# The experts' first product by one level of Strassen's algorithm, in two token blocks with the weights loaded for each

## The chip, the cores and the metric

The kernel runs on one core of one Trainium2 chip. The metric is the device time of one execution in microseconds (us), from the first to the last instruction and what lies around them. A program on one core has no other core to wait for. The profile's engines are PE (TensorE, matmul), PEld (its weight loads, which overlap PE), DVE (VectorE), ACT (ScalarE), POOL (GpSimd) and SP (SyncE, which only issues DMAs here).

## What is computed

Three stages in float32. The first is an attention over a small memory, the second a feed-forward layer whose activation is h·cos(h), the third a dense mixture of four experts. Only the third is changed:

```python
def _moe2_ref(x, domain_probs, w1, w2):      # x [2304, 512], w1 [4, 512, 1024], w2 [4, 1024, 512]
    p = domain_probs / (domain_probs.sum(-1, keepdims=True) + 1e-09)
    out = np.zeros((N, D), dtype=np.float32)
    for e in range(E):                        # E = 4
        h = np.maximum(x @ w1[e], 0.0)
        out += p[:, e:e + 1] * (h @ w2[e])
    return out
```

## The kernel before, in words

PE multiplies in float32 by splitting: every operand is held as a high part of reduced precision (`F32R`) and a low part, the rest. `mm3` (L143 to L147) issues three matmuls for one product, high·high, high·low and low·high, so every product below counts three times. The high part is made by an ACT copy, the low part by a subtraction on DVE or POOL (`split`, L101; `split_w`, L105).

**Stage 1** (attention and first feed-forward layer, some 458 us) ends with a loop over slices of the hidden dimension. For each slice and half-sequence `hidden1` (L327) computes `hp` on PE, then the activation goes through ACT, DVE, ACT, DVE and ACT, and at last POOL makes the low part of the tile `gt` (L103). `output1` (L363) multiplies `gt` by `wo`, and DVE adds the product onto `acc` (L380). The output of a unit is issued two units later, which gives the chain time. `acc` holds all 2304 tokens, transposed (d_model on the partitions), in two halves of 1152 tokens.

**Stage 2** (the experts) cuts the hidden dimension of the four experts into 16 slices of 256 and the tokens into 6 blocks of 384. `x1` holds the split of all six blocks, made from `acc` by 24 ACT copies and 24 DVE subtractions (L103, tile `x`) around the end of stage 1. For each slice and block, 96 units in all, `hidden2` (L469) does 2 (halves of the slice) × 4 (quarters of d_model) × 3 matmuls of 384 columns into `hp`, ACT takes the ReLU as the high part (L484), and DVE makes the low part (L485), both for the whole unit of 768 columns. `output2` (L490) then does 3 token tiles × 2 × 3 matmuls of 512 columns into `op`, and DVE scales each by the expert's probability and adds it onto the output (L507), which lies where `acc` lay. The output of a unit is issued behind the hidden product of the next, so PE has other work while ACT and DVE make `ht`. `hp` has two buffers of two PSUM banks, `op` has two tags of two buffers of one bank each.

`load2` (L455) loads a slice's two weight tiles `wa` and `wb` by DMA into `raw` (L116) and splits each: one ACT copy of 1024 columns (L108) and four low parts of 256 columns on POOL (L110). It is called 16 times, each a whole slice ahead. The first two slices are loaded during stage 1: there the DMAs stand in ACT's queue, held back to certain activations (`issue_after`, the list `marks`), and half the low parts are on DVE.

The order of instructions on each engine is set when the program is built, by a list scheduler with a model of its own, from the order of the code, the buffers and `issue_after`. Every engine then takes its own queue strictly in that order.

Of the kernel before, what the change touches and what calls it, by code (L numbers as in the profile page):

```python
# [9 lines left out]
F32 = mybir.dt.float32  # L10
# [14 lines left out]
def tile_kernel(  # L25
# [36 lines left out]
    ps_o = ctx.enter_context(tc.tile_pool(name="ps_o", bufs=2, space=PSUM))  # L62
    ps_a = ctx.enter_context(tc.tile_pool(name="ps_a", bufs=2, space=PSUM))
    c_ctx = ExitStack()
    ps_h = [c_ctx.enter_context(tc.tile_pool(name="ps_h", bufs=2, space=PSUM))]
    ps_c = c_ctx.enter_context(tc.tile_pool(name="ps_c", bufs=2, space=PSUM))
# [74 lines left out]
                op1=ALU.bitwise_or,  # L141
            )

    def mm3(ps, lt, rt, first, last):
        for i, (a, b) in enumerate(((0, 0), (0, 1), (1, 0))):
            nc.tensor.matmul(  # L146
                out=ps, lhsT=lt(a), rhs=rt(b), start=first and i == 0, stop=last and i == 2  # L147
            )

    cs_ctx = ExitStack()  # L150
# [284 lines left out]
            nu += 1  # L435
    wide[0] = True
    c_ctx.close()
    ps_h[0] = ctx.enter_context(tc.tile_pool(name="ps_h2", bufs=2, space=PSUM, reuse_waits="tile"))
# [11 lines left out]
    for p in pend:  # L450
        output1(*p)
    cs_ctx.close()

    x1b = ctx.enter_context(tc.tile_pool(name="x1b", bufs=1, reuse_waits="tile"))
    hg_p = ctx.enter_context(tc.tile_pool(name="hg", bufs=3, reuse_waits="tile"))  # L455
    x1 = [
        (x1b if i else x1a).tile([128, 2, KD, NB], F32R, tag=f"x1_{i}", name="x1") for i in range(NBLK)
    ]

    def load2(s, eng=nc.sync, after=None):  # L460
        e, f0 = s // SPE, (s % SPE) * FS
# [8 lines left out]
        return tiles  # L470

    def hidden2(i, wa):
        hp = ps_h[0].tile([128, NFC, 512], F32, tag="h", name="hp")
        for fc in range(NFC):
            for kk in range(KD):
                mm3(
                    hp[:, fc, :NB],
                    lambda x: wa[:, x, kk, fc * 128:fc * 128 + 128],
                    lambda x: x1[i][:, x, kk, :],
                    kk == 0,  # L480
                    kk == KD - 1,
                )
        ht = hg_p.tile([128, 2, NFC, NB], F32R, tag="hg", name="ht")
        nc.scalar.activation(out=ht[:, 0], in_=hp[:, :, :NB], func=ACTF.Relu)  # L484
        nc.vector.scalar_tensor_tensor(  # L485
            out=ht[:, 1], in0=hp[:, :, :NB], scalar=0.0, in1=f32(ht[:, 0]), op0=ALU.max, op1=ALU.subtract
        )
        return ht

    def output2(s, i, ht, wb):  # L490
        for tt in range(TPB):
            op = (ps_o, ps_a)[tt % 2].tile([128, DM], F32, tag="oa"[tt % 2], name="op")
# [8 lines left out]
            ti = i * TPB + tt  # L501
# [8 lines left out]
            if s == E * SPE - 1:  # L510
                nc.sync.dma_start(out=out[ti * 128:ti * 128 + 128, :], in_=dst)

    for i in range(NBLK):
        u, o = divmod(i * NB, NT // 2)
        with tc.issue_after(marks[(-3, -2, -1, -1, -1, -1)[i]].ins):
            for d in range(KD):
                split(x1[i][:, 0, d], x1[i][:, 1, d], x1v[:, u, d, o:o + NB])

    units = [(s, i) for s in range(E * SPE) for i in range(NBLK)]
# [12 lines left out]


# [28 lines left out]
```

## Time and profile before

| What | Value |
|---|---|
| median of 3 runs (lowest to highest) | 1261.95 us (1261.72 to 1263.91) |
| span of the profiled execution (the page has no other time of it) | 1260.3 us |
| PE, PEld, DVE, ACT, POOL busy, share of the span | 97%, 87%, 54%, 30%, 19% |
| stage 2, from 480 to 1248 us: PE busy | 768.0 of 768.0 us |
| bytes moved by DMA | 55.98 MB, mean 44 GB/s |

Busy is an average over stages. PE's busy time counts matmuls that overlap in its pipeline, so the distance from the start of one group of matmuls to the start of the next is the better measure of what a matmul costs. An order view (below) shows what stands on an engine's queue behind what, and nothing of durations.

### The profile page before, as it was taken

Reading aid. Unit: us, or ns where it says so; the run is one execution under the profiler, and the core shown is the slowest. Engines: PE = TensorE matmul, PEld = TensorE weight load, DVE = VectorE, ACT = ScalarE, POOL = GpSimd, SP = SyncE. Lnnn points to the kernel's source line nnn. Section 1 sums busy time; section 2 is a strip of 40 time slices with the busy share of each in tenths; the row PEclk is TensorE's granted clock in tenths of the full one; section 3 lists DMA queues with packets and bytes.
Section 4 is the critical chain, followed back from the end, with each engine's and each line's share of the span. In section 5 each row is a group of like instructions: output and inputs, shape, how many; then the busy total and the mean of one; then the engine's idle time right before and its main releaser. Section 6 shows DMA issues by size and latency. Waiting matters only on the chain.

```text
span 1260.3 us, 17964 instructions
## 1 busy us (share of the span) xinstructions
PE 1226.7 (97%) x7562; PEld 1096.5 (87%) x7562; DVE 681.8 (54%) x1139; ACT 380.8 (30%) x594; POOL 242.8 (19%) x253
## 2 busy tenths in 40 slices
PE   7788999999999999999999999999999999999998
PEld 5466799999999999889998999889988999899987
DVE  5798989789778873333333333333333333333333
ACT  2466756566556641111111111111111111111010
POOL 1344433333234410010110100101101001001000
PEclk6689999999999999999999999999999999999999
DMA  9953002102212200010100100001001001010012
GB/s 235 237 126 81 19 35 68 37 33 68 68 35 68 68 2 17 17 34 1 34 17 17 34 17 17 34 1 34 17 18 34 17 17 34 1 34 1 1 43 108
DMA packets 35248, 55.98 MB, mean 44 GB/s; under 512 B 2112, under 2 KB 22624, under 8 KB 35168
## 3 DMA queue, kind: packets, MB, share of 16 engines
q1 hardware_dynamic: 28224, 39.07, 11.3%
q10 hardware_dynamic: 6880, 15.73, 4.0%
q8 instruction: 60, 0.98, 0.3%
q14 instruction: 20, 0.16, 0.0%
q0 software_dynamic: 64, 0.04, 0.0%
HBM read 50.11 MB, written 4.72 MB: 44 GB/s over the span
## 4 chain that ended last, share of the span: by engine, by line
PE 90%; DVE 4%; DMA 4%; ACT 1%; issue 0%; SPq 0%; POOL 0%; ACTq 0%; DVEq 0%
PE op L146 47%; PE hp L146 40%; PE vw_ps L314 2%; DMA phi<-in_phi_dram 2%; DMA raw<-in_moe_w_out_dram 1%; DMA q<-in_q_dram 1%; PE kvp L215 1%; PE pq L208 1%; DVE mx L183 1%; DVE gt L103 0%; DVE y L359 0%; DVE kk L354 0%; DVE st L272 0%; DVE wi L135 0%; DVE acc L380 0%
## 5 line engine op out<-in xcount | busy, mean ns | idle before, releaser
L146 PE MATMUL op<-wb,ht 128*128 128x512 f32 x1728 | 418.0, 395 | 1.1 <-ACT ht L484 1.1
L146 PE MATMUL hp<-x,wa 128*128 128x384 f32 x2304 | 416.2, 336 | 0.0
L146 PEld LDWEIGHTS hp<-x,wa 128*128 128x128 f32 x2304 | 402.7, 188 | 8.6
L146 PEld LDWEIGHTS op<-wb,ht 128*128 128x128 f32 x1728 | 323.5, 188 | 70.3 <-ACT ht L484 1.3
L485 DVE SCALAR_TENSOR_TENSOR ht<-hp,ht 128x768 fp32r<-128x768 f32 x96 | 91.9, 958 | 400.0 <-ACT ht L484 400.0
L484 ACT ACTIVATE ht<-hp 128x768 fp32r<-128x768 f32 x96 | 77.8, 812 | 632.3 <-PE hp L146 632.3
L507 DVE SCALAR_TENSOR_TENSOR acc<-op,p_all,acc 128x512 f32<-128x512 f32 x270 | 201.9, 748 | 89.3 <-PE op L146 89.3
L146 PE MATMUL op<-gt,wo 128*128 128x288 f32 x1536 | 227.6, 298 | 3.2 <-DVE vw L103 2.0
L146 PEld LDWEIGHTS op<-gt,wo 128*128 128x128 f32 x1536 | 211.0, 189 | 8.8 <-DVE gt L103 1.9
L110 POOL TENSOR_TENSOR wa<-raw,wa 128x256 fp32r<-128x256 f32 x60 | 43.4, 754 | 507.4 <-ACT wa L108 507.4
L146 PE MATMUL hp<-attnT,vw 128*128 128x288 f32 x768 | 130.4, 305 | 5.2 <-DVE y L359 2.8
L146 PEld LDWEIGHTS hp<-attnT,vw 128*128 128x128 f32 x768 | 110.5, 192 | 18.8 <-issue 12.8
L103 POOL TENSOR_TENSOR gt<-y,gt 128x576 fp32r<-128x576 f32 x52 | 80.5, 1547 | 174.2 <-ACT gt L102 143.2
L380 DVE TENSOR_TENSOR acc<-op,acc 128x288 f32<-128x288 f32 x224 | 96.3, 449 | 19.6 <-PE op L146 19.2
L110 POOL TENSOR_TENSOR wb<-raw,wb 128x256 fp32r<-128x256 f32 x60 | 43.2, 751 | 132.7 <-ACT wb L108 132.7
L358 ACT ACTIVATE y<-y 128x576 f32<-128x576 f32 (+1 forms) x76 | 46.2, 609 | 64.4 <-DVE y L350 51.3
L102 ACT ACTIVATE gt<-y 128x576 fp32r<-128x576 f32 (+1 forms) x76 | 46.0, 606 | 38.2 <-DVE y L359 38.0
L359 DVE TENSOR_TENSOR y<-hp,y 128x576 f32<-128x576 f32 (+1 forms) x76 | 49.6, 653 | 5.9 <-ACT y L358 5.8
L347 ACT ACTIVATE y<-hp 128x576 f32<-128x576 f32 (+1 forms) x76 | 42.9, 568 | 14.4 <-PE hp L146 14.1
L350 DVE SCALAR_TENSOR_TENSOR y<-kk,y 128x576 f32<-128x576 f32 x52 | 42.4, 815 | 4.8 <-ACT kk L349 4.2
L314 PE MATMUL vw_ps<-wi,vz 128*32 128x256 f32 x512 | 37.2, 401 | 2.1 <-DVE wi L135 2.1
L349 ACT ACTIVATE kk<-y 128x576 f32<-128x576 f32 x52 | 35.6, 685 | 1.4
(82 smaller groups left out, 617.0 us busy)
## 6 DMA issues: line engine op xcount, KB each, us to landing
raw<-in_moe_w_dram SPq DMA_DIRECT2D x28, 512.0 KB, 3.5
raw<-in_moe_w_out_dram ACTq DMA_DIRECT2D x14, 512.0 KB, 3.5
raw<-in_moe_w_in_dram ACTq DMA_DIRECT2D x12, 512.0 KB, 3.7
kv<-in_k_dram SPq DMA_DIRECT2D x16, 288.0 KB, 5.6
kv<-in_v_dram SPq DMA_DIRECT2D x16, 288.0 KB, 6.8
q<-in_q_dram SPq DMA_DIRECT2D x8, 576.0 KB, 7.6
out_dram<-acc SPq DMA_DIRECT2D x18, 256.0 KB, 2.0
phi<-in_phi_dram SPq DMA_DIRECT2D x8, 288.0 KB, 7.8
```

What stands on the lines that cost most here:

```text
L102: nc.scalar.activation(out=hi, in_=src, func=ACTF.Copy)
L103: (eng or nc.vector).tensor_tensor(out=lo, in0=src, in1=f32(hi), op=ALU.subtract)
L110: (nc.vector if early and c % 512 else nc.gpsimd).tensor_tensor(out=t[:, 1, c:c + 256], in0=src[:, c:c + 256], in1=f32(t[:, 0, c:c + 256]) ...
L146: nc.tensor.matmul(out=ps, lhsT=lt(a), rhs=rt(b), start=first and i == 0, stop=last and i == 2)
L314: nc.tensor.matmul(out=vw_ps[32 * i:32 * i + 32, g, :], lhsT=vz[b][:, g, i, :], rhs=wi[:, 2 * g + i // 2, :], start=True, stop=True,)
L347: marks.append(nc.scalar.activation(out=y, in_=hv, func=ACTF.Copy, scale=INV_2PI, bias=0.25))
L358: nc.scalar.activation(out=y, in_=y, func=ACTF.Sin, scale=-TWO_PI if wide[0] else TWO_PI)
L359: nc.vector.tensor_tensor(out=y, in0=hv, in1=y, op=ALU.mult)
L380: nc.vector.tensor_tensor(out=dst, in0=op[:, :TH], in1=dst, op=ALU.add)
L484: nc.scalar.activation(out=ht[:, 0], in_=hp[:, :, :NB], func=ACTF.Relu)
L485: nc.vector.scalar_tensor_tensor(out=ht[:, 1], in0=hp[:, :, :NB], scalar=0.0, in1=f32(ht[:, 0]), op0=ALU.max, op1=ALU.subtract)
L507: nc.vector.scalar_tensor_tensor(out=dst, in0=op, scalar=pe, in1=dst, op0=ALU.mult, op1=ALU.add)
```

## The change

Tokens: instead of six blocks of 384, the tokens are taken as two blocks (u) of 1152, and all 16 slices are run for the first block before the second begins. So the weights are loaded and split 32 times instead of 16. Each block has two groups (j) of 512 and 640 tokens; a unit is one slice and one group, 64 units in all.

Products: for a unit the group's tokens are halved (n = 256 or 320), d_model is halved, and the slice is halved. The 2×2×2 half-size products, 8 by the direct way, are made from 7 by Strassen's algorithm in Winograd's form. The seven left operands of a slice (three quarters of the weights and four combinations) are made in `load2`: four POOL subtractions and seven low parts, all of 256 columns on POOL, three ACT copies. The seven right operands of a group (three quarters of x and four combinations) are made by `build_x`: four DVE combinations, seven ACT copies, seven DVE low parts, each of 2n columns. The sums are taken on the way out: ACT copies the first product out of PSUM, DVE does five additions, and two products are accumulated in PSUM onto banks (`ba`, `b5`) that were already read once. The ReLU and the low parts are taken in three pieces.

PSUM: `hp` and `op` get pools of their own, 5 banks for products and 3 for outputs, in place of the four kinds above.

The diff, cut to its core:

```diff
-    def mm3(ps, lt, rt, first, last):
+    def mm3(ps, lt, rt, first, last, more=False):
...
-    x1a = ctx.enter_context(tc.tile_pool(name="x1a", bufs=1, side="right", reuse_waits="tile"))
...
+    SUBS = ((0, 256), (512, 320))
+    xp = ctx.enter_context(tc.tile_pool(name="xp", bufs=1, reuse_waits="tile"))
+    tp = ctx.enter_context(tc.tile_pool(name="tp", bufs=2, reuse_waits="tile"))
+    hg_p = ctx.enter_context(tc.tile_pool(name="hg", bufs=2, reuse_waits="tile"))
+
+    def build_x(u, j, after=None):
+        t0, n = SUBS[j]
+        xv = x1v[:, u]
+        a11, a12 = xv[:, 0:2, t0:t0 + n], xv[:, 2:4, t0:t0 + n]
+        a21, a22 = xv[:, 0:2, t0 + n:t0 + 2 * n], xv[:, 2:4, t0 + n:t0 + 2 * n]
...
+        def put(o, src):
+            x = xp.tile([128, 2, 2, n], F32R, tag=f"x{j}_{o}", name=f"x{j}_{o}")
+            nc.scalar.activation(out=x[:, 0], in_=src, func=ACTF.Copy)
+            nc.vector.tensor_tensor(out=x[:, 1], in0=src, in1=f32(x[:, 0]), op=ALU.subtract)
+            ops[o] = x
+
+        with tc.issue_after(after.ins) if after else nullcontext():
+            put(0, a11)
+            s1 = comb("sA", a21, a22, ALU.add, nc.vector)
+            s2 = comb("sB", s1, a11, ALU.subtract, nc.vector)
+            put(5, s2)
+            s3 = comb("sC", a11, a21, ALU.subtract, nc.vector)
+            put(6, s3)
+            put(4, s1)
+            put(3, a22)
+            put(1, a12)
+            s4 = comb("sA", a12, s2, ALU.subtract, nc.vector)
+            put(2, s4)
...
     def load2(s, eng=nc.sync, after=None):
...
+            pool.tensor_tensor(out=tt[:, 0], in0=b12, in1=b11, op=ALU.subtract)
+            pool.tensor_tensor(out=tt[:, 1], in0=b22, in1=tt[:, 0], op=ALU.subtract)
+            pool.tensor_tensor(out=tt[:, 2], in0=b22, in1=b12, op=ALU.subtract)
+            pool.tensor_tensor(out=tt[:, 3], in0=b21, in1=tt[:, 1], op=ALU.subtract)
...
+            for o, src in enumerate((b11, b21, b22, tt[:, 0], tt[:, 1], tt[:, 2], tt[:, 3])):
+                pool.tensor_tensor(out=wa[:, 1, o], in0=src, in1=f32(wa[:, 0, o]), op=ALU.subtract)
...
+    PROD = {1: (0, 0), 2: (1, 1), 3: (2, 2), 4: (6, 3), 5: (3, 4), 6: (4, 5), 7: (5, 6)}
...
+        ba = bank()
+        prod(ba, 1)
+        p1 = tmp("p1")
+        nc.scalar.copy(out=p1, in_=ba[:, :n])
+        b6 = bank()
+        prod(b6, 6)
+        u2 = tmp("u2")
+        add(u2, b6, p1)
+        b7 = bank()
+        prod(b7, 7)
+        u3 = tmp("u3")
+        add(u3, b7, u2)
+        b5 = bank()
+        prod(b5, 5)
+        add(c[:, 1, n:], b5, u3)
+        b4 = bank()
+        prod(b4, 4)
+        add(c[:, 0, n:], b4, u3)
+        prod(ba, 2, True)
+        nc.scalar.activation(out=ht[:, 0, 0, :n], in_=ba[:, :n], func=ACTF.Relu)
...
+        prod(b5, 3, True)
+        add(c[:, 1, :n], b5, u2)
...
+    units = [(u, s, j) for u in range(NU) for s in range(NS2) for j in range(2)]
...
+    ps_p = ctx.enter_context(tc.tile_pool(name="ps_p", bufs=5, space=PSUM, reuse_waits="tile"))
+    ps_q = ctx.enter_context(tc.tile_pool(name="ps_q", bufs=3, space=PSUM, reuse_waits="tile"))
+    for u, s, j in units:
+        q_ = u * NS2 + s
+        if j == 1 and 0 < q_ < NU * NS2 - 1:
+            w[q_ + 1] = load2((q_ + 1) % NS2)
+        ht = hidden2(j, xo[u, j], w[q_][0])
+        if u + 1 < NU and s == NS2 - 1:
+            xo[u + 1, j] = build_x(u + 1, j)
```

Three places of the order follow. Numbers behind a name tell buffers apart; line numbers of the change are its own.

**PE in the middle of stage 2.** Before, a unit is one run of 24 matmuls for `hp` and three output tiles of the unit ahead:

```order
L146 MATMUL hp_5823<-x1_5331,wa_5401 128x384 x24
L146 MATMUL op_5851<-wb_5409,ht_5796 128x512 x6
L146 MATMUL op_5859<-wb_5409,ht_5796 128x512 x6
L146 MATMUL op_5867<-wb_5409,ht_5796 128x512 x6
L146 MATMUL hp_5875<-x1_5332,wa_5401 128x384 x24
```

Now a unit of the larger group (`x1_0` to `x1_6` are its seven right operands):

```order
L147 MATMUL hp_6192<-x1_0_5358,wa_5941 128x320
L147 MATMUL hp_6201<-x1_5_5365,wa_5941 128x320 x2
L147 MATMUL op_6156<-wb_5732,ht_5965 128x512 x6
L147 MATMUL hp_6201<-x1_5_5365,wa_5941 128x320 x4
L147 MATMUL hp_6210<-x1_6_5370,wa_5941 128x320 x6
L147 MATMUL hp_6219<-x1_4_5373,wa_5941 128x320 x6
L147 MATMUL hp_6227<-x1_3_5376,wa_5941 128x320 x6
L147 MATMUL hp_6192<-x1_1_5379,wa_5941 128x320 x6
L147 MATMUL op_6254<-wb_5958,ht_6061 128x512 x6
L147 MATMUL op_6262<-wb_5958,ht_6061 128x512 x6
L147 MATMUL hp_6219<-x1_2_5384,wa_5941 128x320 x6
L147 MATMUL op_6270<-wb_5958,ht_6061 128x512 x6
```

Between the fifth product (into `hp_6219`, the bank `b5`) and the last, which accumulates onto that bank, stand two products and two output tiles.

**DVE at the handover from stage 1 to stage 2.** Before, the low parts of the first blocks stand among the last additions onto `acc`; these are the rows around the last four of them:

```order
L380 TENSOR_TENSOR acc_73<-op_5288,acc_73 128x288
L380 TENSOR_TENSOR acc_73<-op_5296,acc_73 128x288
L103 TENSOR_TENSOR x1_5333<-acc_73,x1_5333 128x384
L380 TENSOR_TENSOR acc_73<-op_5304,acc_73 128x288
L103 TENSOR_TENSOR x1_5334<-acc_73,x1_5334 128x384
L380 TENSOR_TENSOR acc_73<-op_5312,acc_73 128x288
```

Now all of `build_x` stands behind the last addition:

```order
L386 TENSOR_TENSOR acc_73<-op_5309,acc_73 128x288
L476 TENSOR_TENSOR sA_5332<-acc_73 128x512
L476 TENSOR_TENSOR sC_5339<-acc_73 128x512
L484 TENSOR_TENSOR x0_0_5329<-acc_73,x0_0_5329 128x512
L476 TENSOR_TENSOR sB_5334<-sA_5332,acc_73 128x512
L484 TENSOR_TENSOR x0_3_5347<-acc_73,x0_3_5347 128x512
L484 TENSOR_TENSOR x0_1_5350<-acc_73,x0_1_5350 128x512
L484 TENSOR_TENSOR x1_0_5358<-acc_73,x1_0_5358 128x640
L484 TENSOR_TENSOR x1_3_5376<-acc_73,x1_3_5376 128x640
L484 TENSOR_TENSOR x1_1_5379<-acc_73,x1_1_5379 128x640
L484 TENSOR_TENSOR x0_4_5344<-sA_5332,x0_4_5344 128x512
L484 TENSOR_TENSOR x0_6_5341<-sC_5339,x0_6_5341 128x512
```

The first product waits for `x0_0`, which has moved behind two combinations; before, its operands were ready long ahead of the last addition.

**POOL near the end of stage 1**, where it also makes the low part of every `gt`. Before:

```order
L110 TENSOR_TENSOR wa_5401<-raw_5399,wa_5401 128x256 x2
L103 TENSOR_TENSOR gt_4904<-y_4902,gt_4904 128x576
L103 TENSOR_TENSOR gt_4971<-y_4969,gt_4971 128x576
L110 TENSOR_TENSOR wb_5409<-raw_5407,wb_5409 128x256 x2
L103 TENSOR_TENSOR gt_5026<-y_5024,gt_5026 128x576
```

Now (`gt_4901`, `gt_4968` and `gt_5023` are the same three tiles; three combinations of `tt_5415` stand ahead of the first row):

```order
L527 TENSOR_TENSOR wa_5416<-raw_5413,wa_5416 128x256 x3
L516 TENSOR_TENSOR tt_5415<-raw_5413,tt_5415 128x256
L104 TENSOR_TENSOR gt_4901<-y_4899,gt_4901 128x576
L527 TENSOR_TENSOR wa_5416<-tt_5415,wa_5416 128x256 x4
L104 TENSOR_TENSOR gt_4968<-y_4966,gt_4968 128x576
L513 TENSOR_TENSOR tt_5714<-raw_5712 128x256
L515 TENSOR_TENSOR tt_5714<-raw_5712 128x256
L514 TENSOR_TENSOR tt_5714<-raw_5712,tt_5714 128x256
L111 TENSOR_TENSOR wb_5433<-raw_5431,wb_5433 128x256 x2
L516 TENSOR_TENSOR tt_5714<-raw_5712,tt_5714 128x256
L104 TENSOR_TENSOR gt_5023<-y_5021,gt_5023 128x576
```

The combinations of the third slice (`tt_5714`) have moved in front of `gt_5023`, and their `raw_5712` shares its buffer with `raw_5413`.

## Rows read from the trace of the kernel before

**Rows 1.** Windows by stage: busy us, instructions, clock (PEclk), DMA share, GB/s.
```profile
30.00:60.00 30.00, 22.75 (x187) 14.94 (x179) 23.84 (x53) 14.27 (x30) 12.05 (x15) 0.57 0.95 231
...
458.00:480.00 22.00, 20.93 (x111) 18.88 (x110) 12.32 (x22) 6.43 (x12) 0.00 (x0) 1.00 0.00 1
480.00:1248.00 768.00, 768.00 (x3861) 693.75 (x3860) 286.72 (x368) 102.07 (x119) 79.23 (x112) 1.00 0.07 23
```

**Rows 2.** Chain that ended last, first and last units: start us, us, what.
```profile
483.14 4.24 PE hp L146 x24
487.38 4.19 PE op L146 x18
...
1243.86 4.16 PE hp L146 x24
1248.02 8.41 PE op L146 x36
```

**Rows 3.** Timeline of PE, 222 to 227 us: start us, us, engine line op.
```profile
222.62 3.35 PE L146 MATMUL op<-gt,wo 128*128 128x288 f32 x24
225.81 0.96 PE L146 MATMUL hp<-attnT,vw 128*128 128x288 f32 x6
```

**Rows 4.** Timeline of PEld and PE, 104 to 128 us: six transposes.
```profile
122.39 0.60 PEld L208 LDWEIGHTS pq<-ident,q 96*128 96x128 f32 x6
122.52 0.66 PE L208 MATMUL pq<-ident,q 96*128 96x96 f32 x6
```

**Rows 5.** Page, part 5: weight loads of the experts' first product.
```profile
L146 PEld LDWEIGHTS hp<-x,wa 128*128 128x128 f32 x2304 | 402.7, 188 | 8.6
```

**Rows 6.** Groups on DVE by line, 100 to 460 us.
```profile
L380 DVE TENSOR_TENSOR acc<-op,acc 128x288 f32<-128x288 f32 x222 | 95.4, 449 | 19.6 <-PE op L146 19.2
L135 DVE SCALAR_TENSOR_TENSOR wi<-raw 128x512 uint32<-128x512 uint32 x12 | 14.5, 1217 | 0.3
L135 DVE SCALAR_TENSOR_TENSOR wf<-raw 128x512 uint32<-128x512 uint32 x12 | 8.2, 687 | 0.2
```

**Rows 7.** Page, part 5: DVE's largest groups in stage 2.
```profile
L485 DVE SCALAR_TENSOR_TENSOR ht<-hp,ht 128x768 fp32r<-128x768 f32 x96 | 91.9, 958 | 400.0 <-ACT ht L484 400.0
...
L507 DVE SCALAR_TENSOR_TENSOR acc<-op,p_all,acc 128x512 f32<-128x512 f32 x270 | 201.9, 748 | 89.3 <-PE op L146 89.3
```

**Rows 8.** Groups on POOL by line: 395 to 435 us, then 480 to 1248 us.
```profile
L103 POOL TENSOR_TENSOR gt<-y,gt 128x576 fp32r<-128x576 f32 x8 | 11.6, 1444 | 12.2 <-issue 12.2
L110 POOL TENSOR_TENSOR wb<-raw,wb 128x256 fp32r<-128x256 f32 x4 | 3.7, 950 | 5.6 <-ACT wb L108 5.6
...
L110 POOL TENSOR_TENSOR wa<-raw,wa 128x256 fp32r<-128x256 f32 x56 | 39.7, 741 | 502.8 <-ACT wa L108 502.8
```

**Rows 9.** Timeline of PE at the handover.
```profile
445.89 4.33 PE L146 MATMUL hp<-x,wa 128*128 128x384 f32 x24
...
453.26 3.46 PE L146 MATMUL hp<-x,wa 128*128 128x384 f32 x19
...
457.95 2.80 PE L146 MATMUL op<-gt,wo 128*128 128x288 f32 x20
461.82 0.50 PE L146 MATMUL op<-wb,ht 128*128 128x512 f32 x1 [1.07 <-ACT ht L484]
```

**Rows 10.** Timeline of DVE, 457 to 466 us: low parts of `x`.
```profile
464.21 1.95 DVE L103 TENSOR_TENSOR x<-acc,x 128x384 fp32r<-128x384 f32 x4
```

**Rows 11.** Timelines, 415 to 462 us: ACT, POOL, then PE.
```profile
420.94 1.06 ACT L108 ACTIVATE wa<-raw 128x1024 fp32r<-128x1024 f32 x1 [1.40 <-DMA raw<-in_moe_w_dram]
...
423.89 1.43 POOL L103 TENSOR_TENSOR gt<-y,gt 128x576 fp32r<-128x576 f32 x1
...
427.08 3.35 PE L146 MATMUL op<-gt,wo 128*128 128x288 f32 x24
...
437.83 3.36 PE L146 MATMUL op<-gt,wo 128*128 128x288 f32 x24
```

**Rows 12.** Page, part 6: loads of the experts' weights in stage 2.
```profile
raw<-in_moe_w_dram SPq DMA_DIRECT2D x28, 512.0 KB, 3.5
```

More of the change, by code (lines that the diff above doesn't have):

```diff
@@ L142, in narrow @@
             )
-    def mm3(ps, lt, rt, first, last):
+    def mm3(ps, lt, rt, first, last, more=False):
         for i, (a, b) in enumerate(((0, 0), (0, 1), (1, 0))):
             nc.tensor.matmul(
-                out=ps, lhsT=lt(a), rhs=rt(b), start=first and i == 0, stop=last and i == 2
+                out=ps,
+                lhsT=lt(a),
+                rhs=rt(b),
+                start=first and i == 0,
+                stop=last and i == 2,
+                skip_group_check=more,
             )
@@ L437, in tile_kernel @@
     c_ctx.close()
-    ps_h[0] = ctx.enter_context(tc.tile_pool(name="ps_h2", bufs=2, space=PSUM, reuse_waits="tile"))
+    ps_h[0] = p_ctx.enter_context(tc.tile_pool(name="ps_h2", bufs=2, space=PSUM, reuse_waits="tile"))
     load_probs()
@@ L470, in load2 @@
[L470 to L487, printed above, removed]
-        return ht
@@ L490, in output2 @@
-    def output2(s, i, ht, wb):
-        for tt in range(TPB):
-            op = (ps_o, ps_a)[tt % 2].tile([128, DM], F32, tag="oa"[tt % 2], name="op")
+        early = after is not None
+        raw = wc.tile([128, KD, FS], F32, tag="raw", name="raw")
+        with tc.issue_after(after[0].ins) if early else nullcontext():
+            eng.dma_start(out=raw, in_=w1[e, :, f0:f0 + FS].rearrange("(k p) f -> p k f", p=128))
+        b11, b12 = raw[:, 0:2, 0:128], raw[:, 0:2, 128:256]
+        b21, b22 = raw[:, 2:4, 0:128], raw[:, 2:4, 128:256]
@@ new lines, in load2, with hidden2, prod, bank @@
+        with tc.issue_after(after[1].ins) if early else nullcontext():
+            wb = load_split("wb", w2[e, f0:f0 + FS, :].rearrange("(k p) d -> p k d", p=128), [NFC, DM], eng, early)
+        return wa, wb
+    PROD = {1: (0, 0), 2: (1, 1), 3: (2, 2), 4: (6, 3), 5: (3, 4), 6: (4, 5), 7: (5, 6)}
+    def hidden2(j, xo, wa):
+        n = SUBS[j][1]
+        def prod(bank, i, more=False):
+            wo_, xo_ = PROD[i]
+            for kk in range(2):
+                mm3(
+                    bank[:, :n],
+                    lambda x: wa[:, x, wo_, kk, :],
+                    lambda x: xo[xo_][:, x, kk, :],
+                    not more and kk == 0,
+                    kk == 1,
+                    more,
+                )
+        def bank():
+            return ps_p.tile([128, 512], F32, tag="p", name="hp")
+        def tmp(tag):
+            return tp.tile([128, n], F32, tag=tag, name=tag)
+        def add(out, ps, sb):
+            nc.vector.tensor_tensor(out=out, in0=ps[:, :n], in1=sb, op=ALU.add)
+        c = tp.tile([128, NFC, 2 * n], F32, tag="c", name="c")
+        ht = hg_p.tile([128, 2, NFC, 2 * n], F32R, tag="hg", name="ht")
+        ba = bank()
[18 more added lines that the diff above has]
+        nc.scalar.activation(out=ht[:, 0, 0, :n], in_=ba[:, :n], func=ACTF.Relu)
+        nc.vector.scalar_tensor_tensor(
+            out=ht[:, 1, 0, :n], in0=ba[:, :n], scalar=0.0, in1=f32(ht[:, 0, 0, :n]), op0=ALU.max, op1=ALU.subtract
+        )
+        prod(b5, 3, True)
+        add(c[:, 1, :n], b5, u2)
+        for fc, lo in ((0, n), (1, 0)):
+            nc.scalar.activation(out=ht[:, 0, fc, lo:], in_=c[:, fc, lo:], func=ACTF.Relu)
+            nc.vector.scalar_tensor_tensor(
+                out=ht[:, 1, fc, lo:],
+                in0=c[:, fc, lo:],
+                scalar=0.0,
+                in1=f32(ht[:, 0, fc, lo:]),
+                op0=ALU.max,
+                op1=ALU.subtract,
+            )
+        return ht
@@ L493, in output2 @@
+    def output2(u, s, j, ht, wb):
+        t0, n = SUBS[j]
+        for tt in range(2 * n // 128):
+            op = ps_q.tile([128, DM], F32, tag="q", name="op")
             for fc in range(NFC):
@@ L509, in output2 @@
                 )
-            if s == E * SPE - 1:
+            if s == NS2 - 1:
                 nc.sync.dma_start(out=out[ti * 128:ti * 128 + 128, :], in_=dst)
[L513 to L519, printed above, removed]
+    xo = {(0, j): build_x(0, j, marks[(-3, -1)[j]]) for j in range(2)}
+    units = [(u, s, j) for u in range(NU) for s in range(NS2) for j in range(2)]
     w = {}
```

49 lines of the change are left out of this document (29 added, 20 removed).

## The prediction

> **What bounds the kernel now.** The windows by stage come first [rows 1]. From 480 to 1248 us PE is busy for all of 768.00 us at a granted clock of 1.00, which is its 2.4 GHz level, while DVE works 286.72, ACT 102.07 and POOL 79.23 us and the DMA engines 7%. The reader is to see there that no other engine is near PE, and that the only loss nearby is 1.07 us between 458 and 480. The chain of work that ended last [rows 2] says the same in order of time: `hp`, `op`, `hp`, `op`, each released by the one before. From the `hp` at 483.14 to that at 1243.86 are 91 units of 8.36 us; `op` takes 4.19 of them, so `hp` 4.17. So stage 2 is a sum of matmul distances. Fewer columns shorten it one for one, every new wait of PE lengthens it one for one, and the 480 to 690 us that DVE, ACT and POOL are idle there are what the change can spend.
>
> **The products.** A matmul of 384 columns costs 4.17/24 = 173.8 ns, one of 512 columns 4.19/18 = 232.8 ns. Stage 1 has a third width [rows 3]: 24 matmuls of 288 columns in 225.81 − 222.62 = 3.19 us, 132.9 ns each. At 2.4 GHz 384 and 288 columns alone would take 160 and 120 ns, so about 13 ns stay on each matmul whatever its width. The line through these two has 0.426 ns a column; it gives 146.5 ns for 320 columns (between two rows) and 119.3 ns for 256, which no row shows. For 256 the bounds are 106.7 ns (the columns alone) and 132.9 ns (no shorter than 288). I take 119.3, because the 13 ns are the same at both narrow widths. Weight loads are no floor above that: six transposes with loads of 128 columns finish in 0.66 us, at most 110 ns each [rows 4].
>
> Removed: 96 × 4.17 = 400.3 us. Added: 32 slices × 7 products × 6 matmuls × (119.3 + 146.5 ns) = 1344 × 265.8 = 357.2 us. That is **−43.1 us** (bounds −60 and −25). The output keeps its 1728 matmuls of 512 columns: 0.
>
> Weight loads are busy for 693.75 of the 768 us [rows 1], and those of this product for 402.7 us in 2304 loads, 174.8 ns each [rows 5]. The Trainium skill (Perfetto Trace Analysis, Identifying the Most-Contended Engine) says to judge how near TensorE is to its limit by just this share and not by the matmuls' busy time. If these loads were the limit, 2688 of them would take 469.8 us, and the term would be +69.5 instead of −43.1. Against it stand the 24 loads of rows 3, one every 132.9 ns, so I keep −43.1.
>
> **In the middle of stage 2** PE gets new partners. A slice now lasts 11.2 us (products) plus 54 × 232.8 ns = 12.6 us (outputs), 23.7 us. DVE's work in it: five additions per unit at 449 ns for 288 columns [rows 6], scaled by columns 5 × (0.40 + 0.50) = 4.5 us; low parts of 4 × 576 columns at 958/768 = 1.25 ns a column, 2.9 us; nine output additions of 748 ns, 6.7 us [rows 7]. Together 14.1 of 23.7 us. POOL's 15 operations of 741 ns [rows 8] are 11.1 us, and their result is wanted a slice later. The one close wait is the bank `b5`: its second product may start only when DVE has read the first. Between them stand two products and two output tiles, 2 × 0.72 + 2 × 1.40 = 4.2 us for the smaller group, against one addition of 0.4 us. So I cost it at 0; the cover is those 4.2 us, and each us beyond it would cost 64 us. An output tile takes 1.40 us, its evacuation 0.75, so three banks are enough.
>
> **The handover.** Before, two whole `hp` units stood among the last outputs of stage 1 [rows 9] and hid the end of its activation chain, all but the 1.07 us. Now no product can start before DVE has finished the last addition onto `acc` and then two combinations and the low part of `x0_0`, and DVE's queue for the first slice holds 22 operations of 512 or 640 columns. Four of 384 columns took 1.95 us [rows 10], 1.27 ns a column: 0.65 and 0.81 us, 16 us in all. Going through the two queues from the end of the last addition (t = 0, PE idle since −0.65): `x0_0` is ready at 1.95, PE waited 2.6. Product 6 wants the high part of `x0_5`, behind `sB` and an ACT copy, 3.15: 0.5. PE then has three single matmuls, products 4 and 2, until 4.95; the low part of `x0_4` stands behind three operations of 640 columns and is ready at 6.95: 2.0. With products 5, 7, 6 and the first products of the second group PE reaches 12.0; the high part of `x1_5` is ready at 14.95: 2.9. Its low part, 17.1, costs another 1.1. After that DVE stays ahead. Sum 9.1 us, against 1.07 before: **+8.0 us**. Bounds: +1.5 (only the first wait is real) and +15 (nothing of the 16 us is hidden). The idle could also bring the clock down: between 30 and 60 us, with PE busy for 22.75 of 30, the granted clock was 0.57 [rows 1]; that is inside the upper bound.
>
> **The end of stage 1.** POOL made 4 low parts per slice of weights there, now 13 operations; beside a busy DVE one takes 950 ns [rows 8]. Before, the weights of the second slice were there at 420.94, the low part of `gt` for the output at 427.08 was made from 423.89 to 425.3, 1.8 us early [rows 11]. Now seven operations, 6.7 us, stand ahead of it: from 421.3 to 428.0, and with its own 1.44 us 429.4, 2.1 us late. Four more end at 433.1. Only then is `raw` free for the third slice, whose load takes 3.5 us [rows 12], and POOL's queue waits for it with six operations ahead of `gt_5023`: 436.7 + 5.7 + 1.4 = 443.8. The output that wants it starts at 437.83 [rows 11], now 2.1 later, and can do two or three matmuls on the high part: 440.2. So 3.6 more, **+5.7 us** (bounds 0 and 12).
>
> DVE's operation on `wi`, always beside POOL, takes 1217 ns, the same on `wf` 687 [rows 6], and POOL's own 950 against 741 [rows 8]. The Trainium skill (SBUF — State Buffer, SBUF: two separate sides) says that a VectorE operation with two SBUF inputs and a GpSimd operation lock each other out of a shared port for a whole instruction. By that, some of the longer POOL queue would also delay DVE's part of the activation chain, about 3 us in all, and the term would be 8.7; in the middle of stage 2, at most four such operations a slice would leave DVE at 17 of 23.7 us. I keep 5.7.
>
> **The second block.** Its `build_x` (16 us of DVE) falls into some 31 us of PE work that bring DVE some 18 us of their own, but three of the combinations are made ahead. I take **+1 us** (0 to 5). The end is unchanged: 1260.3 less the last matmul's 1256.43 [rows 2].
>
> **Sum.** −43.1 + 8.0 + 5.7 + 1 = −28.4. From the span of 1260.3 that is 1231.9; the median of the runs lies 1.65 above that span, so **1233.5 us**. From no change a measurement here tells about 0.2%, 2.5 us.
>
> **Rivals.**
> - *The distance does not fall below that of 288 columns.* 256 columns at 132.9 ns: the products cost 375.5, the sum is −10.1, 1252 us. For it: no row is narrower at full clock with this operand. Against: the equal 13 ns and rows 4.
> - *The edges are nearly free*, since list order lets POOL and DVE catch up: handover +1.5, the others 0. The sum is −41.6, 1220 us. Against: the queues are strict, and their lengths are counted.
> - *Slower: PE waits on `b5` in each unit.* If DVE's queue comes so late that the addition ends more than 4.2 us after product 5, every unit waits. It decides from 28.4/64 = 0.45 us per unit; at 1 us the time is 1233.5 + 64 = 1297. For it: DVE's queue interleaves output additions with the chain, and POOL can hold it up. Against: 14.1 of 23.7 us, and 10 times the time needed.
> - *Slower by the loads.* At 174.8 ns a load the sum is +84, 1344 us. Rows 3 speak against.
>
> **Chances.** The forecast, with its edges anywhere from half to one and a half of what I took (1226 to 1241) and the distance within some 5 ns, 70%. Narrow floor 10%. Free edges 10%. Waits on `b5` 7%, loads 2%, others 1%. The range 1217 to 1254 takes in the first three. Faster by over 0.2%: 88%. Within it: 3%, the narrow floor with dear edges. Slower: 9%.
>
> **What would show it.** Right: 32 × 42 matmuls of 256 and 320 columns at 119 and 146 ns start to start, PE busy without a gap from some 490 us to the end but for a us near the middle, idle PE of 9 us behind the last stage-1 output with DVE's `x` tiles named, and idle PE before outputs near 427 and 440 us with POOL's `gt` named. Wrong: one distance for both widths; a gap in every unit with a releaser on DVE; or no gap at the edges.

## The result, and the profile after

The changed kernel takes 1223.49 us (median of 4 runs, 1220.88 to 1227.39), the kernel before 1261.84 us in the same comparison. The ratio is 0.9703, with a 95% interval of 0.9678 to 0.9728: 38.4 us less, where 28.4 were forecast. The profiled execution has a span of 1222.8 us, against 1260.3 before.

The first 300 us differ by some us from profile to profile. So the parts are compared from a fixed point, the start of the 24th activation from the end of stage 1 (ACT, L347 before and L353 now, at 319.61 and 319.13 us; between 317.0 and 325.9 us in the thirteen profiles of this case). From there the span lasts 940.7 us before and 903.7 us now, 37.0 less. A second profile of the changed kernel gives 902.8, so this measure is good to about 1 us. Where a stretch is measured to or from an addition, its start is meant.

**Steady state.** The page's lines of the changed kernel on PE's busy time and on the loads of the first product. PE is busy for 97% as before; the product has 2688 loads and as many matmuls, before 2304 [rows 5]:

```profile
PE 1189.1 (97%) x7946; PEld 1055.3 (86%) x7946; DVE 868.3 (71%) x1571; ACT 486.4 (40%) x854; POOL 525.3 (43%) x609
...
L147 PEld LDWEIGHTS hp<-x,wa 128*128 128x128 f32 x2688 | 381.2, 189 | 25.8 <-DVE x L484 3.0
```

The chain of work that ended last, of the changed kernel, one slice (start us, us, what):

```profile
589.81 2.80 PE op L147 x12
592.61 0.88 PE hp L147 x6
...
603.29 0.70 PE hp L147 x6
...
613.47 2.80 PE op L147 x12
```

It is PE all the way, as in [rows 2]. A slice lasts 613.47 − 589.81 = 23.66 us. Six matmuls of 320 columns take 0.88 us, 147 ns each, six of 256 take 0.70, 117 ns each.

**The handover.** The same chain where stage 1 ends:

```profile
449.36 3.05 PE op L147 x21
452.41 0.02 issue
452.43 0.46 DVE acc L386
452.89 0.60 DVE sA L476
453.49 0.60 DVE sC L476
454.09 0.60 DVE x L484
...
465.19 0.74 DVE sB L476
465.93 0.02 issue
465.95 0.75 ACT x L483
466.70 0.04 issue
466.74 6.18 PE hp L147 x30
```

Here the chain leaves PE: from 452.43 to 465.93 us it goes through DVE's queue. Between the fixed point and PE's last matmul it does so only once more, for one addition of 0.47 us at 448.84. PE's timeline in that stretch names what it waited for (idle us and releaser in brackets; five waits, 4.40 us in all, of which two rows). The third row is ACT's, ahead of the copy `p` that the second wait names: ACT, too, was waiting for DVE.

```profile
454.74 0.85 PE L147 MATMUL hp<-x,wa 128*128 128x256 f32 x5 [2.01 <-DVE x L484]
...
465.39 1.16 PE L147 MATMUL hp<-x,wa 128*128 128x320 f32 x6 [1.32 <-ACT p L564]
...
464.29 0.74 ACT L483 ACTIVATE x<-sA 128x640 fp32r<-128x640 f32 x1 [1.66 <-DVE sA L476]
```

In windows (columns as in [rows 1]), and behind them one slice:

```profile
455.00:460.00 5.00, 4.12 (x23) 3.63 (x23) 5.00 (x9) 1.28 (x3) 0.00 (x0) 0.69 0.00 0
460.00:465.00 5.00, 4.07 (x26) 3.44 (x25) 5.00 (x9) 2.09 (x4) 0.00 (x0) 0.97 0.00 0
465.00:470.00 5.00, 4.41 (x18) 4.04 (x19) 5.00 (x10) 2.56 (x6) 0.00 (x0) 0.71 0.00 0
470.00:475.00 5.00, 5.00 (x36) 4.87 (x35) 4.50 (x10) 1.17 (x3) 0.00 (x0) 0.95 0.01 3
613.47:637.13 23.66, 23.66 (x139) 21.21 (x139) 14.72 (x25) 6.50 (x13) 11.41 (x15) 1.00 0.15 45
```

DVE is busy throughout, and the granted clock, 1.00 until 455 us, fell behind the waits to 0.69 and 0.71, that is to 1.2 GHz for a part of these windows. That is 5 × (0.31 + 0.03 + 0.29 + 0.05) = 3.4 us of PE's full speed. In the second profile of the change the waits are 4.34 us and the clock takes only 5 × (0.07 + 0.27) = 1.7 us, from 450 to 460 us.

**The end of stage 1.** POOL's timeline, then SP's (the issue of the third slice's load), then PE's (two outputs):

```profile
419.48 0.74 POOL L513 TENSOR_TENSOR tt<-raw 128x256 f32<-128x256 f32 x1 [0.61 <-DMA raw<-in_moe_w_dram]
...
424.89 1.44 POOL L104 TENSOR_TENSOR gt<-y,gt 128x576 fp32r<-128x576 f32 x1
...
431.00 0.73 POOL L513 TENSOR_TENSOR tt<-raw 128x256 f32<-128x256 f32 x1
...
436.17 1.44 POOL L104 TENSOR_TENSOR gt<-y,gt 128x576 fp32r<-128x576 f32 x1
...
424.96 0.38 SPq L506 DMA_DIRECT2D raw<-in_moe_w_dram  x1
...
426.47 3.34 PE L147 MATMUL op<-gt,wo 128*128 128x288 f32 x24
...
437.20 3.63 PE L147 MATMUL op<-gt,wo 128*128 128x288 f32 x24
```

The low parts are ready at 426.33 and 437.61. The first is in time by 0.14 us. The second is late by 0.41, but the output can begin on the high part, and its 24 matmuls take only 0.27 us longer than before [rows 11].

**The sum**, from the fixed point: products −45.5 (32 × 23.66 = 757.1 for 96 × 8.36 = 802.6), end of stage 1 +0.1 (133.3 us to the last addition; before 141.6, with 8.4 of stage 2's products among it), handover +7.8 (766.5 us from the last addition to PE's end less 757.1 and less the middle, 8.9, against 1.07 before), middle +0.5. Together −37.1. Of the 8.9 us of the handover the waits and the clock make 7.8.

### The profile page after: what moved, and what is told of

Read it like the earlier page. It is cut to its first block, busy times and chain, and to the rows that moved or that the text cites. A ratio compares the mean times of both kernels' runs of the same rounds, so it can differ in the third digit from the quotient of the medians.

```text
span 1222.8 us, 20022 instructions
## 1 busy us (share of the span) xinstructions
PE 1189.1 (97%) x7946; PEld 1055.3 (86%) x7946; DVE 868.3 (71%) x1571; ACT 486.4 (40%) x854; POOL 525.3 (43%) x609
## 4 chain that ended last, share of the span: by engine, by line
PE 89%; DVE 6%; DMA 3%; ACT 1%; issue 0%; POOL 0%; SPq 0%; DVEq 0%
PE op L147 48%; PE hp L147 37%; PE vw_ps L320 2%; DMA phi<-in_phi_dram 2%; DMA q<-in_q_dram 1%; PE kvp L221 1%; DMA raw<-in_moe_w_out_dram 1%; DVE x L484 1%; PE pq L214 1%; DVE mx L189 1%; DVE gt L104 0%; DVE y L365 0%; DVE st L278 0%; DVE acc L386 0%; DVE kk L360 0%
## 5 line engine op out<-in xcount | busy, mean ns | idle before, releaser
L147 PE MATMUL op<-wb,ht 128*128 128x512 f32 x1728 | 439.3, 396 | 0.0
L147 PEld LDWEIGHTS hp<-x,wa 128*128 128x128 f32 x2688 | 381.2, 189 | 25.8 <-DVE x L484 3.0
L147 PE MATMUL hp<-x,wa 128*128 128x320 f32 (+1 forms) x2688 | 394.2, 296 | 4.4 <-DVE x L484 2.5
L111 POOL TENSOR_TENSOR wb<-raw,wb 128x256 fp32r<-128x256 f32 x124 | 90.1, 758 | 225.5 <-ACT wb L109 225.4
L587 ACT ACTIVATE ht<-c 128x256 fp32r<-128x256 f32 (+3 forms) x128 | 72.0, 562 | 285.7 <-DVE c L557 285.7
L588 DVE SCALAR_TENSOR_TENSOR ht<-c,ht 128x256 fp32r<-128x256 f32 (+3 forms) x128 | 95.2, 743 | 63.5 <-ACT ht L587 63.5
L527 POOL TENSOR_TENSOR wa<-raw,wa 128x256 fp32r<-128x256 f32 x96 | 71.6, 773 | 150.1 <-ACT wa L517 150.1
L557 DVE TENSOR_TENSOR c<-hp,u 128x256 f32<-128x256 f32 (+1 forms) x192 | 87.4, 457 | 42.3 <-PE hp L147 37.9
L527 POOL TENSOR_TENSOR wa<-tt,wa 128x256 fp32r<-128x256 f32 x128 | 108.1, 875 | 0.0
L564 ACT COPY p<-hp 128x256 f32<-128x256 f32 x64 | 25.6, 400 | 109.5 <-PE hp L147 109.4
```

Of the source, the lines that this page charges most:

```text
L111: (nc.vector if early and c % 512 else nc.gpsimd).tensor_tensor(out=t[:, 1, c:c + 256], in0=src[:, c:c + 256], in1=f32(t[:, 0, c:c + 256]) ...
L147: nc.tensor.matmul(out=ps, lhsT=lt(a), rhs=rt(b), start=first and i == 0, stop=last and i == 2, skip_group_check=more,)
L527: pool.tensor_tensor(out=wa[:, 1, o], in0=src, in1=f32(wa[:, 0, o]), op=ALU.subtract)
L557: nc.vector.tensor_tensor(out=out, in0=ps[:, :n], in1=sb, op=ALU.add)
L587: nc.scalar.activation(out=ht[:, 0, fc, lo:], in_=c[:, fc, lo:], func=ACTF.Relu)
L588: nc.vector.scalar_tensor_tensor(out=ht[:, 1, fc, lo:], in0=c[:, fc, lo:], scalar=0.0, in1=f32(ht[:, 0, fc, lo:]), op0=ALU.max, op1=ALU.su ...
```

## The experiments

All are edits of the changed kernel; from the combinations on POOL on, a run keeps edits of earlier runs, as its expectation says, and its cut shows the new ones alone. "Handover" is the time from the last addition of stage 1 to the first ReLU of slice 3, the slices counted from 0 (the expectations call it the third slice); 77.3 and 76.3 us in the two profiles of the change.

### Eight products in place of seven

```diff
-        prod(ba, 1)
-        p1 = tmp("p1")
...
+        for fc in range(NFC):
+            for h in range(2):
+                hp = bank()
+                for kk in range(KD):
+                    mm3(
+                        hp[:, :n],
+                        lambda x: wa[:, x, kk, fc * 128:fc * 128 + 128],
+                        lambda x: xo[2 * h + kk // 2][:, x, kk % 2, :],
+                        kk == 0,
+                        kk == KD - 1,
+                    )
```

> All 8 half-size products in place of 7, with the same two token blocks, widths, banks and twice loaded weights, and no combinations. If the gain of the change is the products that it saves (A), a slice has 96 product matmuls for 84: at the 117 and 147 ns measured in the change, 32 x 12 x 132 ns = +50.7 us in stage 2, and some 4 us less at the handover, since only 8 low parts are made there: about 1269 us, 0.5% above the kernel before. If the gain came from the new order of blocks, banks or tiles and not from the saved products (B), the time stays near the change's 1223 us. The idle PE at the handover should fall below 3 us with this shorter DVE queue.

Measured: 1274.33 us (1.0107 of before, 1.0081 to 1.0133). Its chain, the first row of one slice and the same row of the next, and the one wait of its PE at the handover:

```profile
610.63 4.20 PE op L147 x18
...
635.88 4.20 PE op L147 x18
```

```profile
454.90 1.33 PE L147 MATMUL op<-gt,wo 128*128 128x288 f32 x4 [6.57 <-ACT gt L103]
```

A slice lasts 25.25 us, 1.59 more than with seven products, 50.9 us in 32 slices. So theory A holds: the gain is the saved products. The new blocks and widths alone cost 32 × 25.25 − 802.6 = +5.4 us; leaving out the eighth product gives 50.9 back. The expectation missed at the handover: ACT's queue had the eight copies of `x`, and DVE's the eight low parts, ahead of the last unit's activation chain, and PE waited 6.6 us for that.

### Narrower and wider products

```diff
-    SUBS = ((0, 256), (512, 320))
+    SUBS = ((0, 192), (384, 384))
```

To make room, the tile `c` loses its unused quarter, and two small constants of stage 1 move to a pool that is released.

> The change, with groups of 384 and 768 tokens in place of 512 and 640, so the half-size products have 192 and 384 columns. If a matmul costs a fixed share per column (A: 117 ns for 256, 147 for 320, 173.8 for 384 are all 0.45 to 0.46 ns a column), 192 columns take 88 ns and the time stays within 2 us of the change's. If some 13 ns stay on each matmul whatever its width (B, the prediction's reading), 192 columns take 93 ns and 384 some 173: the same sum, told apart by the distance alone. If the loads of 128 columns set a floor near the 110 ns that the transposes bound (C), 1344 matmuls take 110 for 88 ns: +30 us, 1252.

Measured: 1254.83 us (0.9962, 0.9944 to 0.998). Its chain:

```profile
600.34 3.33 PE hp L137 x30
...
604.39 0.65 PE hp L137 x6
...
622.27 1.04 PE hp L137 x6
...
624.94 3.33 PE hp L137 x30
```

Six matmuls of 192 columns take 0.65 us, 108 ns each, and 30 take 3.33, 111 ns each; 384 columns take 1.04/6 = 173 ns. A slice lasts 24.60 us, 0.94 more: 30 us in all, the size that C gave. From 256 columns on the price is proportional: 0.456 ns a column at 256, 0.458 at 320, 0.451 at 384. At 192 the distance is 108 to 111 ns in place of the 88 that this would give, so the products of the change, at 117 ns, stand just above it.

That the load of the weights sets this distance is argued, not shown: no run changed the load alone. The Trainium skill (TensorE: Matmul & The Clock Gate, LDWEIGHTS (loading the stationary operand)) gives a load of P columns as P/1.2 ns whatever the rows, an estimate of 107 for 128: the products of this run come close to it. But the six transposes of [rows 4], each with a load of 128 columns in 96 rows, do not agree: one matmul of theirs lasts 0.25 us, so six in 0.66 us start (0.66 − 0.25)/5 = 0.082 us apart. A load of 128 columns does not hold every matmul to 107 ns.

The weight loads' busy share, which the Trainium skill (Perfetto Trace Analysis, Identifying the Most-Contended Engine) takes as a measure, does not tell the two apart: 21.21 of 23.66 us (90%) in the change, 22.23 of 24.60 (90%) here, where half of the products stand some 20 ns farther apart than their columns would give.

### More work on POOL at the end of stage 1

```diff
+            for _ in range(2 if early else 0):
+                pool.tensor_tensor(out=tt[:, 2], in0=b22, in1=b12, op=ALU.subtract)
+                pool.tensor_tensor(out=tt[:, 3], in0=b21, in1=tt[:, 1], op=ALU.subtract)
```

> Four more POOL subtractions (some 0.71 us each, the same values written again) in the two loads of weights during stage 1, ahead of the low parts of the output's tile gt. If POOL's queue is as close to what PE waits for there as the change's trace looks (low part ready at 426.33 for an output at 426.47, and at 437.61 for one at 437.20) (A), 2.8 us more cost 2 to 3 us at each of two or three outputs, +5 to +9 us in all. If the queue has slack that the walk missed (B), the time stays within 1 us.

Measured: 1227.06 us (0.9729, 0.9703 to 0.9756); from the fixed point to the last addition 137.9 us in place of 133.3, +4.6. PE's timeline shows idle time where there was none:

```profile
415.75 0.37 PE L147 MATMUL op<-gt,wo 128*128 128x288 f32 x1 [1.91 <-DVE acc L386]
...
439.73 0.37 PE L147 MATMUL op<-gt,wo 128*128 128x288 f32 x1 [0.72 <-DVE acc L386]
```

The size fits A, a little under its 5 to 9; from the fixed point to the end it is 3.6 us, since the handover is 76.3. The chain that ended last ran on PE there in the change, but for the one addition; here POOL's low parts and combinations are its largest part from 424 to 451 us. But PE did not wait for `gt`, as A had it. The releaser is DVE's addition, which frees the output's bank, and ahead of it stands an operation of the activation that took 1.96 us, with POOL busy beside it; the shortest of its kind in the change took 0.74:

```profile
413.27 1.96 DVE L356 SCALAR_TENSOR_TENSOR y<-kk,y 128x576 f32<-128x576 f32 x1
```

PE's two waits are 2.63 us. Behind the first the granted clock was 0.67 from 415.8 to 421 us, some 1.7 us of full speed, so both make 4.3 of the 4.6 us. The program's order around these outputs changed with the edit, so the single waits are not laid at one tile's door.

### The bank b5, freed later

```diff
-        add(c[:, 1, n:], b5, u3)
+        for _ in range(5):
+            add(c[:, 1, n:], b5, u3)
```

> The addition that frees bank b5 for its second product is made five times in place of once, 64 times over. DVE gets 4 x (0.37 + 0.44) = 3.2 us more in a slice, 18 of 23.7 us, and the bank is free 1.5 to 1.8 us later. If the cover of 4.2 us between the two products on that bank holds (A), the time stays within 2.5 us of the change's 1223. If the bank or DVE's queue is close to what PE waits for (B), each unit is longer by up to 1.6 us, +100 us; 0.2 us a unit would already be +13.

Measured: 1226.29 us (0.9721, 0.9695 to 0.9748). In the window from 520 to 800 us:

```profile
520.00:800.00 280.00, 280.00 (x1636) 250.99 (x1635) 206.55 (x389) 77.51 (x141) 134.75 (x176) 1.00 0.15 46
```

DVE does 206.55 us of work where the change has 174.56, and PE is still busy for all of 280.00; a slice lasts 23.64 us. A holds: in the steady state the cover is there. From the fixed point it is 2.4 us more, of which 1.1 lie at the second block, where DVE also builds the new `x`.

### Work for PE in the first wait

```diff
+    end1 = mm[0]
...
+    idle = ps_q.tile([128, DM], F32, tag="q", name="idle")
+    with tc.issue_after(end1.ins):
+        for _ in range(9):
+            nc.tensor.matmul(out=idle[:, :128], lhsT=ones, rhs=ones, start=True, stop=True)
```

> The change, with nine matmuls of 128 columns on constants put into PE's queue behind the last matmul of stage 1, that is into the 2.0 us in which PE waits for the first low part of x. Their result is not used. If the 3.4 us that the lower clock costs behind the handover (granted 0.69 to 0.97 from 455 to 475 us) are a cost of their own, brought by the idle PE (A), the clock stays up and the time falls by some 3 us. If DVE's queue sets the end of the handover (B), PE gets faster only to wait longer for the next low parts: more idle time, a higher clock, the same end within 1 us.

Measured: 1221.88 us (0.9692, 0.9662 to 0.9721). Windows, then PE's timeline:

```profile
455.00:460.00 5.00, 3.49 (x24) 3.15 (x25) 5.00 (x9) 0.79 (x3) 0.00 (x0) 1.00 0.00 0
...
465.00:470.00 5.00, 4.34 (x29) 4.26 (x30) 4.87 (x10) 2.29 (x4) 0.00 (x0) 1.00 0.02 3
```

```profile
458.55 0.86 PE L149 MATMUL hp<-x,wa 128*128 128x256 f32 x5 [1.31 <-DVE x L487]
...
465.66 3.76 PE L149 MATMUL hp<-x,wa 128*128 128x320 f32 x25 [1.61 <-ACT x L486]
```

The clock stays at 1.00, so it was the idle PE that brought it down. Of the 3.4 us, 1.9 come back (handover 75.3 for 77.3), or 1.0 of 1.7 against the second profile; the rest turns into longer waits for `x` (the two rows, 1.31 for 0.46 and 1.61 for 0.20). Both theories are half right: DVE's queue sets most of the end, the clock a part. In the time of the whole run the intervals overlap with the change's, so no gain is shown there.

### The first operands built earlier

```diff
+    bx0 = build_x(0, 0)
+    next(bx0)
+    for p in pend:
+        output1(*p)
+    cs_ctx.close()
```

The first part of `build_x` (`x0_0`, `x0_5`, `x0_6`, and by the scheduler's choice all four combinations) uses buffers of stage 1 that are free earlier (`cw`).

> The change, with the first three right operands of the first group (x0_0, x0_5, x0_6) and the four combinations that they come from built ahead of the last two outputs of stage 1, in buffers of stage 1 that are free earlier. If DVE's queue behind the last addition is what PE waits for (A), the first three waits (2.0 + 0.4 + 0.5 us) go, PE is not idle at first and the clock falls less: 4 to 6 us faster than the change, 1217 to 1219 us. If the queue only moves its end (B), the wait comes at the operands of the second group and 1 us or less is won.

Measured: 1222.92 us (0.9723, 0.9703 to 0.9743). The first product now starts at once, but PE's timeline has a new wait:

```profile
461.33 1.15 PE L137 MATMUL hp<-x,wa 128*128 128x320 f32 x6 [1.88 <-DVE u L567]
```

The handover is 74.9 us, 2.4 less, but stage 1 is 1.7 longer (135.0). That DVE's new operations delay the activation chain of the last units there is tested below (`tail[0]`). From the fixed point 902.6 us: B. DVE's work had only been moved.

### Combinations on POOL, the second block held back

```diff
+        ceng = nc.gpsimd if u == 0 and j else nc.vector
...
-            xo[u + 1, j] = list(build_x(u + 1, j))[-1]
+            xo[u + 1, j] = list(build_x(u + 1, j, last[0]))[-1]
```

> As the one before, and the combinations of the second group (x1) on POOL, which is idle there, and DVE's combinations of the second token block held back to the end of the first block, so that DVE's queue at the handover loses seven more operations, some 5 us. If that queue is the cause (A), PE's idle time at the handover falls to 1 us or less, the clock stays near 1.0 and 6 to 7 us of the 7.4 are won: 1216 to 1217 us. If POOL's slower combinations are late (B), PE waits for x1 tiles and no more is won than by the run before.

Measured: 1228.85 us (0.9754, 0.9739 to 0.977), slower than the change. DVE's timeline, then POOL's:

```profile
454.11 1.78 DVE L484 TENSOR_TENSOR x<-t,x 128x512 fp32r<-128x512 f32 x1
455.82 4.00 DVE L484 TENSOR_TENSOR x<-acc,x 128x512 fp32r<-128x512 f32 x2
459.74 0.68 DVE L484 TENSOR_TENSOR x<-t,x 128x512 fp32r<-128x512 f32 x1
```

```profile
455.30 2.01 POOL L474 TENSOR_TENSOR sC<-acc 128x640 f32<-128x640 f32 x1
457.27 2.00 POOL L474 TENSOR_TENSOR sB<-sA,acc 128x640 f32<-128x640 f32 x1
```

While POOL works, each low part on DVE lasts as long as one operation of POOL, 1.8 to 2.0 us; as soon as POOL stops, 0.68. So three operations that left DVE cost it 3.8 us. The Trainium skill (SBUF — State Buffer, SBUF: two separate sides) says that such a pair locks a shared port for the whole instruction: this run agrees. Holding the second block's combinations back to its end cost 4.3 us there, where the change loses 0.5 and the run before nothing. Neither theory had that.

### Only the second block held, and the order of DVE's queue

Combinations are on DVE again; the second block's are held behind the first scaling of an output. The second run also holds the second group's operands, but for `x1_0`, behind the first unit's additions:

```diff
-            xo[u + 1, j] = list(build_x(u + 1, j, last[0]))[-1]
+            xo[u + 1, j] = list(build_x(u + 1, j, first[0]))[-1]
...
+            xo[0, 1] = list(build_x(0, 1, sums[0]))[-1]
```

> As x0_early (DVE makes all combinations again, none on POOL), but DVE's combinations of the second token block are held behind the first scaling of an expert's output, so five operations of 0.6 to 0.73 us, 3.2 us in all, leave DVE's queue at the handover; they have the whole first block to be made in. If DVE's queue sets the end of the handover (A), the time from the last addition of stage 1 to the third slice falls by 2 to 3 us, from 74.9 us in x0_early to 72 to 73 (77.3 in the change), and the middle stays free of a wait: about 1217 us. If PE waits there for the products' own chain (B), it stays within 0.7 us of x0_early.

> As the run before, and the operands of the second group, but for x1_0, are held behind the first unit's additions on DVE, so that the additions come first, then the second group's combinations and low parts. In x0_early PE waited 1.9 us behind such an addition, which stood behind four low parts of 640 columns. If the order within DVE's queue is what costs (A), another 1 to 2 us go: 71 us from the last addition to the third slice, about 1216. If the sum of DVE's work is what costs, whatever its order (B), the wait moves to x1 tiles and the time stays within 0.7 us of the run before.

Measured: 1224.31 us (0.9708, 0.9686 to 0.9731) and 1223.31 us (0.9698, 0.966 to 0.9736); handovers of 72.7 and 72.6 us, 900.4 and 900.1 from the fixed point. The first is A by its size: five operations less on DVE, some 3.2 us, and a handover 2.25 us shorter. What it gained is mostly the clock. PE's waits there fell only from 3.55 to 2.96 us, 0.6; but in `x0_early` the granted clock was 0.84 and 0.82 from 460 to 470 us, 1.7 us of full speed, and with the shorter waits it stayed at 1.00. Together that is 2.3 us. The second is B: the order within the queue is worth nothing.

### Less built ahead, against the change on the same chip

```diff
-    bx0 = build_x(0, 0)
+    bx0 = build_x(0, 0, tail[0])
```

Here `tail[0]` is the last multiplication of stage 1's activation chain; only `x0_0` and `x0_5` are made ahead, the rest behind the last addition.

> As early_u2_first, but only x0_0, x0_5 and their two combinations are made ahead, and not before the last unit's activation chain is through DVE; the rest of the first group stands behind the last addition. In early_hold_block2 and early_u2_first stage 1 itself became longer by 1.6 to 1.8 us (135.1 and 134.9 us from the 24th activation from the end to the last addition, 133.3 in the change), because DVE's early work delayed the chain of the last units. If that is the cause (A), 133.5 us come back there, the handover keeps its 72.6 us, and from that activation to the end it is 898.5 us, 5 less than the change's 903.7. If PE then waits for x0_6 and x0_4 (B), the handover is some 1.5 us longer and nothing is won.

> The changed kernel itself, on the same chip as tail_x0. By the traces tail_x0 should be 5 us faster (A) or the same (B); the part of the run ahead of the first experts' weights differs from run to run by about as much, so the difference of the medians should lie between 0 and 8 us.

Measured: 1222.25 us (0.9693, 0.9675 to 0.9711) and 1224.32 us (0.9717, 0.9699 to 0.9735). Stage 1 is back at 133.5 us, but the handover is 74.4, so from the fixed point 900.6: B. Each version pays for DVE's work at one place or the other. The last three versions gain 2.2 to 3.6 us by the traces, but the intervals overlap with the change's, so none is shown to beat it.

## Why the prediction was right or wrong

**Direction and mechanism: right.** Stage 2 is a sum of matmul distances, and one product in eight less shortens it one for one; the eight-product run shows that the new blocks and widths alone do not. The time, 1223.5 us, lies inside the stated range, which takes in two rivals as well, but below the 1226 to 1241 that the forecast itself was given.

**The products: right in size, wrong in reason.** −45.5 for −43.1. Forecast were 119.3 and 146.5 ns, measured 117 and 147. The step "about 13 ns stay on each matmul whatever its width" failed: the distance is proportional, 0.45 to 0.46 ns a column from 256 to 512, and at 192 it stops at 108 to 111 ns. The line was drawn through two points 96 columns apart, and 32 columns of extrapolation were short enough to do no harm; that was luck, for at 192 columns the same line gives 92 ns, 16 to 19 too few. The two rivals on a floor had it at 132.9 and at 174.8 ns, where none is.

**The middle: right.** DVE is busy 14.72 us in a slice for 14.1 forecast, POOL 11.41 for 11.1, and four more additions on `b5` cost nothing in the steady state.

**The handover: right in size, by two errors.** +7.8 for +8.0 (6.9 in the second profile). DVE's queue is the cause, as forecast: the chain goes through it, and five operations less give 2.25 us (1.7 of these by the clock). But PE idles for 4.4 us, not 9.1. Operations of 512 columns start every 0.60 us and those of 640 every 0.74 (forecast 0.65 and 0.81), and a slower PE comes later to each wait; no run shows the two shares apart. The slower clock, 3.4 us in one profile and 1.7 in the other, had been put only into the upper bound.

**The end of stage 1: the step that failed.** +0.1 for +5.7, 5.6 of the 8.7 us between the forecast sum (−28.4) and the measured one (−37.1). The walk through POOL's queue had the right operations, but started them at 421.3 and took 0.95 us for each, the mean of a group [rows 8] that stood beside two operations of its own kind on DVE (from 410.46 and from 432.13 us in the kernel before). Measured, they start at 419.48. That is 1.2 us earlier against the output that wants `gt` (427.08 before, 426.47 now): the load was there 0.85 us sooner (420.94 and 419.48), and the combinations at the head of the queue, which need `raw` and no ACT copy, began at once. Six of the seven take 0.70 to 0.74 us and one 1.26. So the seven end at 424.89 in place of 428.0, and the low part of `gt` is 0.14 us early in place of 2.1 late.

The walk's second half, 3.6 of the 5.7 us, failed for another reason as well. It let `raw` become free only behind the last four low parts (433.1), but these read `tt` and not `raw`, as the order ahead of the prediction shows (`wa_5416<-tt_5415`). The third slice's load was issued at 424.96, right behind the last combination, and POOL took it up at 431.00 without a wait. That the queue has no slack is real: with four more operations a load, 4.6 us appear. That PE waits there for `gt` itself no run shows.

**The second block:** +0.5 for +1.

**The rivals.** Free edges (1220 us) came nearest by number, but only stage 1's end was free. Waits on `b5`, which would have made it slower, did not come in the steady state even with the bank freed later. The 1344 us of the loads rival lack the 1.65 us that the other sums add: 1346. Of the signs that were named, the two distances and the gapless middle came; the 9 us of idle PE were 4.4, and the idle PE before the outputs near 427 and 440 us did not come.

## What to carry to other kernels

Cost a product that trades width for count by the distance per column, and look for the width at which the distance stops falling: here 256 columns at 117 ns keep the gain, while 192 columns at 108 to 111 ns give back 30 us of it. Walk a strict queue with the duration of an operation beside the neighbours that it will have, and for every buffer find its last reader; here a mean over another stretch was off by a third, and a buffer was free 8 us earlier than the walk had it. At a seam between stages ask which queue holds the first operands: moving its work elsewhere gained little here, and taking 3.2 us of work out of it gained 2.25, most of it because PE's shorter waits left the clock up.

## What had not been expected of the hardware

- The distance of matmuls with a new load of 128×128 weights each, at a granted clock of 1.00 (2.4 GHz): 108 to 111 ns at 192 columns, 117 at 256, 147 at 320, 173 at 384. Transposes of 96 columns, with a load of 96×128, stood 82 ns apart.
- DVE's subtraction of 512 columns took 0.68 us alone and 1.8 to 2.0 us beside POOL's subtraction of 640 columns.
- Two us of idle PE and some short waits were followed by a granted clock of 0.69 over the next 5 us (0.73 in the second profile); with nine small matmuls in the gap it stayed at 1.00.
